# A Fourier-mixing and expert-layer kernel: the planner may hold back VectorE, ScalarE and GpSimd work, any free bank is taken, tile rows are turned in place, h comes in half tiles

## The chip, the cores and the metric

The kernel runs on one core of one Trainium2 chip. The metric is device microseconds of one execution. Three runs of the kernel before gave 1494.55, 1497.58 and 1498.59 us, median 1497.58.

## The reference

```python
X = np.fft.rfft(x, axis=1)                    # x: 8 batches, 2496 positions, 256 columns, float32
Y = X * (filt_r + 1j * filt_i)[None, :, :]
y = np.fft.irfft(Y, n=2496, axis=1)
x = y.reshape(19968, 256)                     # one row per token
logits = x @ w_gate                           # 8 experts
expert_idx = np.argmax(logits, axis=1)
gate_w = softmax(logits)[row, expert_idx]
h = np.maximum(x_of_expert @ w1[e], 0.0)      # 256 -> 1024, each row through its own expert only
out = gate_w[:, None] * (h @ w2[e])           # 1024 -> 256
```

## The kernel before

**The transform.** 2496 = 39 x 64, so each batch is transformed in four stages of matrix products. Stage A (`stage_a`) transforms along 39 with the table `ta` (three blocks of 39 positions on 117 partitions become three blocks of 40 values on 120 partitions); stage B (`stage_b`) transforms along 64 with `tb`, after which VectorE multiplies by the filter; stage C (`stage_c`) goes back along 64 with `tc`; stage D (`stage_d`) goes back along 39 with `td`. Between A and B, and between C and D, the data goes through DRAM (`zd`, `ud`) to be laid out anew, but for the first batch, which is turned on the chip (`first_a`, `turn_z`, `first_c`, `turn_u`). A batch is read in chunks `CH` of up to four columns blocks (22 in all: five chunks of four and one of two). A matmul has 512 columns (two blocks of 256), and its result lies in one of seven PSUM banks (`bank`) until VectorE or ScalarE copies it out (`evac`).

**The routing.** The output `yo` of stage D is turned, multiplied by the gate weights (`turn_y`, then `logits` and `turn_logits` for the first three batches, `block_logits` and `block_back` for the others), and `route` finds each token's expert, its place in that expert's list and its gate. GpSimd then writes each token's row, with its number and gate, into that place of a table `rowsd` in DRAM by indirect DMA (`scatter`), one DMA for the tokens of one block, on up to 117 partitions.

**The experts.** `tile_map` cuts the lists into tiles of 512, 256 or 128 rows. For a tile, `rows_in` loads the rows into `xg`, `turn_x` turns them on VectorE into another tile `xT`, `hidden` (or `hidden_by_quarters`, which does seven products in place of eight, with sums made by GpSimd in `turn_x` and `w1_sums`) makes h in the tile `hT`, and `result` multiplies by w2, scales by the gate and writes the rows of the output by indirect DMA. One `hT` tile holds h of half an expert's w1 columns, and there are three of them.

**The order.** All engines' queues are filled by a planner that runs while the program is built. `Order` keeps an estimated clock for each engine; every instruction goes through `Issue`, which advances the clocks and issues at once, so the line of every instruction in the profile is L238. A main loop picks, by estimated readiness, the next step for TensorE from the list of transform steps (`slot`) or from two streams of expert products (`first_products`, `second_products`, with `when` giving their readiness). After each step it lets stores go (`flush`), issues loads (`more_loads`, `prefetch`), and takes up to four pieces of routing (`side`). For a copy out of a bank, `either` picks VectorE or ScalarE by which would end first, and the copy is put in that engine's queue at once. Buffers, banks too, are taken in rotation (`Slots`). Instructions of one engine execute in the order of its queue.

Of the kernel before, what the change touches and what calls it, by code (L numbers as in the profile page):

```python
# [34 lines left out]
TK = NB * NS  # L35
DH = D // P
# [4 lines left out]
NJ = D // CT  # L41

# [13 lines left out]
def dft_tables():  # L56
# [25 lines left out]
    ids = np.zeros((NB, N1, NG))  # L82
    valid = np.zeros((NB, N1, NG))
    for j in range(NB):
        for i in range(len(range(j, N2, NB))):
            ids[j, :, i] = token(q, NB * i + j)
            valid[j, :, i] = 1.0

    by_block = np.zeros((4, CT, NG + 2))
    by_block.reshape(P, NG + 2)[:TP, :NG] = valid.reshape(TP, NG)  # L90
# [5 lines left out]
        "ta": ta.reshape(TP, TK),  # L96
        "tb": tb,
        "tc": tc,
        "td": np.pad(td.reshape(TK, TP), ((0, 0), (0, P - TP))),
        "sg": np.concatenate([sg[:, :NF // 2], sg[:, NF // 2:]]),  # L100
        "ids": ids.reshape(TP, NG),
        "valid": np.concatenate([np.pad(valid.reshape(TP, NG), ((0, P - TP), (0, 0))), by_block], axis=1),
    }


def lay_x(x):

    out = np.zeros((x.shape[0], P, NG, D), x.dtype)
    q = np.arange(N1)
    for j in range(NB):  # L110
        for i in range(len(range(j, N2, NB))):
            out[:, j * N1:(j + 1) * N1, i] = x[:, token(q, NB * i + j)]
    return out
# [11 lines left out]
class Order:  # L125
# [3 lines left out]
    LOAD = 2.0  # L129

    def __init__(self, nc):
        self.nc = nc
        self.t = dict.fromkeys(("tensor", "vector", "scalar", "gpsimd", "sync", "transfers"), 0.0)
        self.slow = self.busy = self.last = 0.0
        self.done, self.used, self.slots, self.ahead = {}, {}, {}, {}
        self.tensor, self.vector, self.scalar, self.gpsimd, self.sync = (
            Issue(self, name) for name in ("tensor", "vector", "scalar", "gpsimd", "sync"))
# [6 lines left out]

    def ready(self, *aps):
        times = [a for a in aps if isinstance(a, float)]
        return max([0.0] + times + [self.done.get(key, 0.0) for a in aps if not isinstance(a, float) for key in self.parts(a)])
# [29 lines left out]
    def count(self, engine, op, args, named):  # L177
        aps = [a for a in list(args) + list(named.values()) if isinstance(a, bass.AP)]
        if not aps:
            return  # L180
# [6 lines left out]
        at = named.get("out_offset")  # L187
        if at is not None:
            ins.append(at.ap)
        kept = [a for a in ins if a.space != DRAM or a.name[:2] in ("zd", "ud")]  # L190
        free = self.t[engine]
        start = max([free] + [self.ready(a) + (self.HOP if engine != "sync" else 0.0) for a in kept])
        if out is not None:
            start = max(start, self.ahead.pop(out.name, 0.0))
            n = int(np.prod([d[1] for d in out.ap][1:])) if out.space != DRAM else 0
        tail = 0.0
        if op.endswith("dma_start"):
            busy = 1.3 if engine == "gpsimd" else 0.4
            self.t[engine] = start + busy
            took = self.transfer(out, named["in_"])  # L200
            self.t["transfers"] = max(self.t["transfers"], start + busy) + took
            end, tail = self.t["transfers"], self.LOAD
        else:
            if out is None:
                took = 0.02
            elif engine == "tensor":
                if start > self.busy + 1.2:
                    self.slow = start + 3.4
                rows = out.ap[0][1]
                took = max(0.1, 0.00085 * n) if op == "transpose" else max(0.216, 0.00169 * n) if rows > 32 else 0.00045 * n  # L210
                took *= 2.0 if start < self.slow else 1.0
                tail = 0.25
            elif engine == "vector":
                took = 0.15 + n / 960
            elif engine == "scalar":
                took = 0.16 + n / 1200
            else:
                took = 0.2 + n / 480
            end = self.t[engine] = start + took
            if engine == "tensor":  # L220
                self.busy = end
# [4 lines left out]
        self.last = end + tail  # L226


class Issue:
# [3 lines left out]
    def __getattr__(self, op):  # L233
        real = getattr(getattr(self.order.nc, self.name), op)

        def issue(*args, **named):
            self.order.count(self.name, op, args, named)
            return real(*args, **named)  # L238

        return issue  # L240


class Slots:
    def __init__(self, order, pool, bufs):
        self.order, self.pool, self.bufs, self.tiles, self.n = order, pool, bufs, {}, {}

    def free(self, tag, k=0):

        past, n = self.tiles.get(tag, []), self.n.get(tag, 0)
        if len(past) + k < n or k >= n:  # L250
            return 0.0
        name = past[k - n]
        return max(self.order.done.get(name, 0.0), self.order.used.get(name, 0.0)) + 0.1

    def tile(self, shape, dtype, **named):
        new = self.pool.tile(shape, dtype, **named)
        past = self.tiles.setdefault(named.get("tag") or named.get("name"), [])
        n = self.n[named.get("tag") or named.get("name")] = named.get("bufs") or self.bufs
        if len(past) >= n:
            name = past[-n]  # L260
            self.order.ahead[new.name] = max(self.order.done.get(name, 0.0), self.order.used.get(name, 0.0)) + 0.1
        past.append(new.name)
        return new


@with_exitstack
def kernel(
# [39 lines left out]
    TR = E * TE  # L307

# [16 lines left out]
    prow = perm.tile([P, 1], I32, name="prow")  # L325
    need = perm.tile([1, 1], I32, name="need")
    ps = open_pool(ctx, name="ps", bufs=7, space=PSUM)

# [4 lines left out]

    tas = cst.tile([TP, TK], F32, name="tas")
    tbs = cst.tile([P, P], F32, name="tbs")
    tcs = cst.tile([P, P], F32, name="tcs")
    tds = cst.tile([TK, P], F32, name="tds")
# [15 lines left out]
    ids0 = cst.tile([TP, NG], F32, name="ids0")  # L353
    vld = cst.tile([P, 2 * NG + 2], F32, name="vld")
# [8 lines left out]
    def experts_pool():  # L363
        first.close()
# [8 lines left out]
    def either(i, n, on_vector, on_scalar):  # L373

        ready = nc.ready(i)
        if max(t["vector"], ready) + 0.15 + n / 960 <= max(t["scalar"], ready) + 0.16 + n / 1200:
            on_vector()
        else:
            on_scalar()

    def evac(o, i, n):
        either(i, n, lambda: nc.vector.tensor_copy(o, i), lambda: nc.scalar.copy(out=o, in_=i))
# [8 lines left out]
    def load_filters(c):  # L391
        f0, n = FH[c]
        if c == 0:
            nc.sync.dma_start(out=tbs, in_=tb)
# [11 lines left out]
        if c == 0:  # L406
            nc.sync.dma_start(out=tcs, in_=tcm)

    def load_rest():
        nc.sync.dma_start(out=tds, in_=td)  # L410
# [33 lines left out]
    def columns(ap, i0, n):  # L444
# [3 lines left out]
        yield TK, slice(0, m), rows[i0 * TK:(i0 + m) * TK, :].rearrange("(i p) d -> p i d", p=TK)  # L448
        if m < n:
            yield NS, slice(m, n), rows[(NG - 1) * TK:, :].rearrange("(i p) d -> p i d", p=NS)  # L450

    ins, outs, lgs, yts, lands = {}, {}, {}, {}, []
    NIN, YB = 7, 6
# [17 lines left out]
    def by_part(ap):  # L471

        return ap.rearrange("t (c f) d -> (t c) f d", c=2)

# [8 lines left out]
    def load_z(b, c):  # L483
        f0, n = FH[c]
        zi = fin(("z", b, c))
        nc.sync.dma_start(out=zi[:, :n], in_=by_part(zd[b])[:, f0:f0 + n, :])

    def load_u(b, c):
        i0, n = CH[c]
        ui = fin(("u", b, c))  # L490
        for r, m, v in columns(ud[b], i0, n):
            if r == TK:

                v = bass.AP(v.tensor, v.offset, [[D, P]] + [list(k) for k in v.ap[1:]])
                r = P
            nc.sync.dma_start(out=ui[:r, m], in_=v)

    def stage_a(b, c):
        i0, n = CH[c]
        xt = ins.pop(("x", b, c))  # L500
        zo = sb.tile([TK, 4, D], F32, tag="st", name="zo", bufs=4)
        for j in range(0, n, 2):
            p = bank()
            mm(p[:TK, :], lhsT=tas, rhs=xt[:TP, j:j + 2, :], start=True, stop=True)
            evac(zo[:, j:j + 2, :], p[:TK, :].rearrange("p (t d) -> p t d", t=2), 512)
        for r, m, v in columns(zd[b], i0, n):
            move(v, zo[:r, m])
# [3 lines left out]
    def stage_b(b, f):  # L511
# [6 lines left out]
        mm(p, lhsT=tbs, rhs=zi[:, j:j + 2, :], start=True, stop=True)  # L518
# [9 lines left out]
        if b == 0 or b < 3 and not sides:  # L528
            nc.gpsimd.tensor_tensor(ys, ys, yw, op=ALU.add)
        else:  # L530
            nc.vector.tensor_tensor(ys, ys, yw, op=ALU.add)

    def stage_c(b, f):
# [6 lines left out]
        mm(p, lhsT=tcs, rhs=ys, start=True, stop=True)  # L540
        evac(uo[:, j:j + 2, :], p.rearrange("p (i d) -> p i d", i=2), 512)
        if j == 2:
            f0 = f - 2
            move(by_part(ud[b])[:, f0:f0 + 4, :], uo)
# [3 lines left out]
    def stage_d(b, c):  # L548
# [8 lines left out]
        for j in range(0, n, 2):  # L557
            p = bank()
            if i0 + j + 2 < NG:
                mm(p, lhsT=tds, rhs=ui[:TK, j:j + 2, :], start=True, stop=True)  # L560
            else:

                for i, k in enumerate((TK, NS)):
                    mm(p[:, i * D:(i + 1) * D], lhsT=tds[:k, :], rhs=ui[:k, j + i, :], start=True, stop=True)
            evac(yo[:, j:j + 2, :D], p.rearrange("p (i d) -> p i d", i=2), 512)

# [824 lines left out]
```

## Time and profile before

| | |
|---|---|
| median of the three runs | 1497.58 us |
| the profiled execution | 1494.36 us |
| its span, from the first to the last instruction | 1492.7 us |
| mean granted TensorE clock | 0.991 |
| TensorE busy, matmuls | 1451.7 us, 97% |
| VectorE, ScalarE, GpSimd busy | 770.7, 471.8, 733.4 us |
| mean DMA rate | 186 GB/s |
| matmul records | 7396 |

PE is the matmul part of TensorE and PEld its weight loads, DVE is VectorE, ACT ScalarE, POOL GpSimd, SP SyncE, which issues most DMAs. A group of instructions is shown as engine, operation, output<-inputs, shape, count, then its busy time, the mean time of one in ns, and the idle time of the engine just before it with what ended it. Matmul durations overlap, since the next one starts before the last one's end; the distance from start to start tells what one costs. A matmul of float32 appears as two records. A wait line names who waited, for whom, us in total, number of times, and the longest.

### The profile page before, as it was taken

Reading aid. Unit: us, or ns where it says so; the run is one execution under the profiler, and the core shown is the slowest. Engines: PE = TensorE matmul, PEld = TensorE weight load, DVE = VectorE, ACT = ScalarE, POOL = GpSimd, SP = SyncE. Lnnn points to the kernel's source line nnn. Section 1 sums busy time; section 2 is a strip of 40 time slices with the busy share of each in tenths; the row PEclk is TensorE's granted clock in tenths of the full one; section 3 lists DMA queues with packets and bytes.
Section 4 is the critical chain, followed back from the end, with each engine's and each line's share of the span. In section 5 each row is a group of like instructions: output and inputs, shape, how many; then the busy total and the mean of one; then the engine's idle time right before and its main releaser. Section 6 shows DMA issues by size and latency. Waiting matters only on the chain. (4 is left out here: it accounts for less than half of the span.)

```text
span 1492.7 us, 24448 instructions
## 1 busy us (share of the span) xinstructions
PE 1451.7 (97%) x7396; PEld 1148.8 (77%) x7396; DVE 770.7 (52%) x1732; ACT 471.8 (32%) x983; POOL 733.4 (49%) x1053
## 2 busy tenths in 40 slices
PE   8898997999989999999999999999999999999998
PEld 6553555776667777777787888887888889999997
DVE  4667677354577656565764555537344334441110
ACT  4453442333322233222233222222222222223332
POOL 3434455344446656554555756764546455741111
PEclk9999999999999999999999999999999999999999
DMA  9749889678767756474456545545455543456661
GB/s 255 252 152 333 289 306 295 207 258 280 251 182 229 219 157 169 131 239 128 128 152 196 130 117 149 147 139 145 151 178 176 167 146 106 117 187 179 181 179 52
DMA packets 216376, 278.10 MB, mean 186 GB/s; under 512 B 124131, under 2 KB 163708, under 8 KB 216245
## 3 DMA queue, kind: packets, MB, share of 16 engines
q1 hardware_dynamic: 197125, 233.19, 52.7%
q0 software_dynamic: 19120, 43.33, 8.3%
q8 instruction: 62, 1.02, 0.3%
q14 instruction: 69, 0.57, 0.1%
HBM read 196.45 MB, written 80.64 MB: 186 GB/s over the span
## 5 line engine op out<-in xcount | busy, mean ns | idle before, releaser
L238 DVE TENSOR_TENSOR hT<-bank,hT 128x512 f32<-128x512 f32 (+1 forms) x504 | 300.7, 627 | 298.9 <-PE bank L238 183.1
L238 PE MATMUL bank<-w2t,hT 128*128 128x256 f32 x1984 | 447.5, 382 | 1.0 <-DVE hT L238 0.5
L238 PEld LDWEIGHTS bank<-w2t,hT 128*128 128x128 f32 x1984 | 377.6, 191 | 62.9 <-issue 9.5
L238 POOL DMA_INDIRECT out_dram<-ys,ng x161 | 160.7, 998 | 459.7 <-ACT ys L238 183.3
L238 PE MATMUL bank<-xT,w1t 128*128 128x256 f32 (+1 forms) x1728 | 316.7, 329 | 0.3 <-DVE xT L238 0.3
L238 PEld LDWEIGHTS bank<-xT,w1t 128*128 128x128 f32 x1728 | 266.8, 192 | 36.5 <-issue 11.8
L238 ACT ACTIVATE hT<-hT 128x1024 f32<-128x1024 f32 (+1 forms) x144 | 133.9, 958 | 378.7 <-DVE hT L238 374.8
L238 POOL DMA_INDIRECT rows<-yo,row x176 | 180.3, 1025 | 69.0 <-POOL yo L238 36.0
L238 ACT ACTIVATE ys<-bank,ng 128x256 f32<-128x256 f32 x128 | 60.6, 473 | 369.6 <-PE bank L238 297.0
L238 PE MATMUL bank<-sums,wsum 128*128 128x256 f32 (+1 forms) x576 | 135.7, 358 | 2.8 <-DVE hT L238 1.8
L238 PE MATMUL bank<-w2s,hT 128*128 x592 | 132.6, 380 | 0.0
L238 PEld LDWEIGHTS bank<-w2s,hT 128*128 128x128 f32 x592 | 110.5, 191 | 13.6
L238 PEld LDWEIGHTS bank<-sums,wsum 128*128 128x128 f32 x576 | 101.2, 191 | 20.1 <-issue 7.3
L238 DVE TENSOR_TENSOR ys<-bank,ht 128x512 f32<-128x512 f32 x80 | 55.0, 688 | 81.9 <-PE bank L238 77.3
L238 PE MATMUL bank<-fin,tas 117*120 117x512 f32 x154 | 76.9, 620 | 11.9 <-DMA fin<-in_x_dram 11.9
L238 PE MATMUL bank<-fin,tds 120*128 120x512 f32 (+1 forms) x168 | 76.6, 576 | 6.0 <-DMA fin<-ud 6.0
L238 DVE STREAM_TRANSPOSE xT<-xg 128x512 f32<-128x512 f32 (+2 forms) x126 | 57.5, 494 | 44.2 <-PE bank L238 44.2
L238 PE MATMUL bank<-fin,tbs 128*128 128x512 f32 x140 | 72.6, 605 | 2.5 <-DMA fin<-zd 2.5
L238 ACT ACTIVATE hT<-bank 128x128 f32<-128x128 f32 (+1 forms) x192 | 58.1, 304 | 50.1 <-PE bank L238 42.4
L238 PE MATMUL bank<-ys,tcs 128*128 128x512 f32 x140 | 72.7, 604 | 1.0 <-DVE ys L238 1.0
L238 POOL TENSOR_TENSOR wsum<-w1t 128x256 f32<-128x256 f32 x72 | 53.4, 742 | 38.1 <-PE bank L238 36.5
L238 PE MATMUL bank<-xT,wsum 128*128 128x256 f32 (+1 forms) x288 | 68.3, 360 | 0.3 <-DVE hT L238 0.3
(150 smaller groups left out, 1491.5 us busy)
## 6 DMA issues: line engine op xcount, KB each, us to landing
w1t<-in_moe_w_dram SPq DMA_DIRECT2D x126, 512.0 KB
w2t<-in_moe_w_dram SPq DMA_DIRECT2D x68, 512.0 KB
fin<-in_x_dram SPq DMA_DIRECT2D x39, 512.0 KB
fin<-zd SPq DMA_DIRECT2D x35, 512.0 KB
ud<-uo SPq DMA_DIRECT2D x35, 512.0 KB
fin<-ud SPq DMA_DIRECT2D x35, 512.0 KB
zd<-zo SPq DMA_DIRECT2D x35, 480.0 KB
xg<-rows SPq DMA_DIRECT2D x112, 128.0 KB
```

Of the source, the lines that this page charges most:

```text
L238: return real(*args, **named)
```

## The change

- **Holding.** An operation of VectorE, ScalarE or GpSimd is no longer issued at once but kept in a list, with the operations that it must follow. After each TensorE step, `advance` issues all held operations whose estimated start has come, earliest first. Where one can run on two engines (`one_of`: copies, relu, scaling on VectorE or ScalarE; the filter's sum on VectorE or GpSimd), the engine that would end it first is picked then. What an instruction of TensorE or SyncE needs is issued before it. The estimates now count a buffer as not free and a tile as not ready while a held operation touches it.
- **Buffers.** Banks and the transform's input tiles are taken where one is free first, not in rotation. Loads for the experts are issued only when a buffer is free within 0.5 us by the estimate (`soon`). `xg` has three buffers, not two.
- **Tile rows.** `turn_x` turns `xg` in place by one instruction in place of two; `xT` is gone, and matmuls and GpSimd's sums read the rows in pieces of 32.
- **h.** Six `hT` tiles of half the size in place of three. `result` takes the products in the order 0, 1, 4, 5, 6, 7, 2, 3, and may be picked 2.0 us before the third half tile is expected.
- **Stage D.** The tokens of one block lie on 124 partitions instead of 117. `stage_d` makes them by four matmuls of 64 output rows into two banks where it made two matmuls of 128 output rows. Rows without a token get an index past the table's end, which the indirect DMA skips.
- **Folded stages.** A form of stages A and D for batches from `BQ` on, with sums and differences (`fold_x`, `fold_y`). `BQ` is 8, and there are 8 batches. The second tables of `ta`, `tb` and `tc` for it are loaded near the end of the transform.
- GpSimd gets a small memset between two scatters that would stand next to one another (16 in the program).

The diff, cut to its core:

```diff
+    def given(self, engine, op, args, named):
+        if self.caught is not None:
+            self.caught.append((engine, op, args, named))
+            return None
+        if engine in self.HELD and self.hold:
+            self.held.append(Held(self, [(engine, op, args, named)]))
+            return None
+        out, ins = self.operands(op, args, named)
+        self.clear([key for a in ins for key in self.parts(a)], self.parts(out) if out is not None else [])
...
+        made = self.issue(engine, op, args, named)
...
+    def advance(self):
+        while True:
+            free = [(work.begin(), k) for k, work in enumerate(self.held) if not work.behind]
+            begin, k = min(free, default=(self.NEVER, 0))
+            if begin > self.t["tensor"]:
+                return
+            self.held[k].go()
...
     def free(self, tag, k=0):
         past, n = self.tiles.get(tag, []), self.n.get(tag, 0)
+        if tag in self.live:
+            return sorted(self.freed(name, tag) for name in past)[k] if past else 0.0
...
+        if tag in self.live:
+            past = self.tiles.setdefault(tag, [None] * n)
+            k = min(range(n), key=lambda k: self.freed(past[k], tag))
...
-        either(i, n, lambda: nc.vector.tensor_copy(o, i), lambda: nc.scalar.copy(out=o, in_=i))
+        nc.one_of(lambda: nc.vector.tensor_copy(o, i), lambda: nc.scalar.copy(out=o, in_=i))
...
-        if b == 0 or b < 3 and not sides:
-            nc.gpsimd.tensor_tensor(ys, ys, yw, op=ALU.add)
-        else:
-            nc.vector.tensor_tensor(ys, ys, yw, op=ALU.add)
+        sums(ys, ys, yw, ALU.add)
...
     def stage_d(b, c):
...
-        for j in range(0, n, 2):
-            p = bank()
-            if i0 + j + 2 < NG:
-                mm(p, lhsT=tds, rhs=ui[:TK, j:j + 2, :], start=True, stop=True)
-            else:
-                for i, k in enumerate((TK, NS)):
-                    mm(p[:, i * D:(i + 1) * D], lhsT=tds[:k, :], rhs=ui[:k, j + i, :], start=True, stop=True)
-            evac(yo[:, j:j + 2, :D], p.rearrange("p (i d) -> p i d", i=2), 512)
+        m, tds = n // 2, tables["td"]
+        both = [bank()[:, :m * D].rearrange("p (i d) -> p i d", i=m) for _ in range(2)]
+        for h in range(2):
+            last = i0 + n == NG and h == 1
+            for k in range(2):
+                if b < BQ:
+                    rows, cols = slice(0, NS if last else TK), slice(64 * k, 64 * k + 64)
...
+                mm(both[k][64 * h:64 * h + 64], lhsT=tds[rows, cols], rhs=ui[rows, h * m:(h + 1) * m, :], start=True, stop=True)
+        evac(yo[:, :m, :D], both[0], m * D)
+        if b < BQ:
+            evac(yo[:, m:n, :D], both[1], m * D)
...
+    def sums(o, i0, i1, op):
+        nc.one_of(*(lambda on=on: on.tensor_tensor(o, i0, i1, op=op) for on in (nc.vector, nc.gpsimd)))
...
     def turn_x(i):
-        xts[i] = pools["moe"].tile([P, DH, 4 * P], F32, tag="xT", name="xT", bufs=2)
-        for dh in range(DH):
-            nc.vector.transpose(xts[i][:, dh, :n * P].rearrange("p (g r) -> p g r", r=QW), xg[:, :n * NQ, dh, :])
+        xg = xg[:, :n * NQ]
+        nc.vector.transpose(xg, xg)
+        xts[i] = xg.rearrange("p g h r -> p h g r")
...
+    def new_hidden(i):
+        new = pools["moe"].tile([P, 2, 4 * P], F32, tag="hT", name="hT", bufs=6)
+        hs.setdefault(i, []).append(new)
+        return new
...
     def result(i, j):
-        for k in range(FT):
+        for m, k in enumerate((0, 1, 4, 5, 6, 7, 2, 3)):
...
+    def soon(tag):
+        return pools["moe"].free(tag) <= max(t["tensor"], t["sync"]) + 0.5
...
-            return max(ps.free("bank"), nc.ready(*hs[i], *((late["w2s"],) if i >= PLACE else (w2t[2 * i], w2t[2 * i + 1]))))
+            return max(ps.free("bank"), nc.expected(hs[i][2]) - 2.0, nc.ready(hs[i][0], hs[i][1], hs[i][3], *((late["w2s"],) if i >= PLACE else (w2t[2 * i], w2t[2 * i + 1]))))
```

## The prediction, made before the changed kernel ran

> **What bounds the kernel now.** First the page's busy lines and its slices: TensorE is busy for 97% of the span, in nearly every slice, and no other engine passes 52%.
>
> ```profile
> span 1492.7 us, 24448 instructions
> PE 1451.7 (97%) x7396; PEld 1148.8 (77%) x7396; DVE 770.7 (52%) x1732; ACT 471.8 (32%) x983; POOL 733.4 (49%) x1053
> ```
>
> So a better choice of engine for a copy pays only where TensorE stands still, and anything that TensorE does more costs its full price. Second, TensorE's waits in three stretches. They sum to 26.7 us before 260 us (20.8 of it for three kinds of transfers), 5.4 us from 260 to 1000 and 2.7 us after that. The longest are these:
>
> ```profile
> PE bank L238 <- DMA fin<-in_x_dram: 12.3, 6, 6.9
> PE bank L238 <- DMA fin<-ud: 6.0, 1, 6.0
> PE bank L238 <- DVE hT L238: 3.6, 4, 1.8
> PE lt L238 <- DVE yt L238: 3.1, 1, 3.1
> ```
>
> Third, the windows. At 120 to 140 us the DMA engines are full, TensorE is busy for 12.89 of 20 us and the granted clock falls to 0.83, so a wait costs more than itself; from 600 on nothing is left to win.
>
> ```profile
> core 0: us, PE busy (x) PEld busy (x) DVE busy (x) ACT busy (x) POOL busy (x), PEclk, DMA share, GB/s
> ...
> 120.00:140.00 20.00, 12.89 (x27) 5.32 (x26) 11.21 (x24) 6.52 (x15) 6.33 (x11) 0.83 1.02 342
> ...
> 600.00:800.00 200.00, 199.03 (x990) 157.50 (x990) 124.45 (x257) 56.40 (x106) 105.41 (x150) 1.00 0.53 155
> ```
>
> Fourth, two pieces of TensorE's timeline (start, duration, tile, records): one step of `stage_d`, and one visit of `block_logits`, whose matmuls write 32 rows each.
>
> ```profile
> 505.89 1.88 PE L238 MATMUL bank<-fin,tds 120*128 120x512 f32 x4
> 507.61 1.03 PE L238 MATMUL bank<-xT,wsum 128*128 128x256 f32 x4
> ...
> 539.63 1.03 PE L238 MATMUL bank<-sums,w1t 128*128 128x256 f32 x4
> 540.59 0.65 PE L238 MATMUL lt<-yt,wb 128*32 128x128 f32 x16
> 541.16 1.13 PE L238 MATMUL bank<-xT,wsum 128*128 128x256 f32 x4
> 542.13 1.24 PE L238 MATMUL bank<-xT,w1t 128*128 128x256 f32 x5
> ```
>
> Starts are to be read, not durations. A matmul leaves two records. The two matmuls of `stage_d` take 507.61 - 505.89 = 1.72 us, 0.43 a record of 512 columns; four records of 256 columns take 0.86, which makes 0.108 for 128 columns.
>
> **What the change moves, part by part.**
>
> *stage_d in half rows.* This is the one part that gives TensorE more work. A step's two matmuls of 128 output rows become four of 64 output rows (the column index k selects table columns, h the half of the output rows): eight records of 512 columns instead of four. The trace has no such step, so its price is bounded by rows on both sides.
> (a) Stream time, lower end: as now, 1.72 us, if the two halves of the array run at once; less is excluded, since each half still streams four records of 512 columns. The `lt` row is nearest: sixteen records of 128 columns, 16 x 0.108 = 1.73 us one by one, are through in 541.16 - 540.59 = 0.57 us, so the four column groups do run together.
> (b) Upper end: eight records one after another, 3.44 us. Forty steps of 1.72 and eight last ones of 0.86 give 75.7 us more.
> (c) Between: the order. In `lt` a column group's two records stand together and the next group's follow; in `stage_d` four records of one half come before the first of the other. If only one record may wait per half while a later one goes past it, the second half starts two records late: six steps instead of four, 0.86 x 40 + 0.43 x 8 = 37.8 us more.
> (d) Going into the split array and back. Around the `lt` visit, the four `sums,w1t` records take 0.96 us to the next start instead of 0.86, `lt` 0.57 instead of a quarter of 1.73 = 0.43, and the four `xT,wsum` after it 0.97 instead of 0.86: 0.10 + 0.14 + 0.11 = 0.35 us a visit. The order of the built kernel has 48 such steps; two stand together and six lie beside a 32-row visit, which saves one of their two changes of form, so about 44 count: 44 x 0.35 = 15.4 us.
> I take (a) with (d), since `lt` is the only split work on record; (b) and (c) stay for the range.
>
> [...]
>
> *More rows.* 132 transposes of 117 columns become 124 columns: 7 x 0.00084 x 132 = 0.8 us. The 66 `wg` matmuls grow as much on a quarter of the array, 0.2 us. With the shorter last step's extra evacuation nothing more than 0.3 us: together 1.3 us.
>
> *Tile rows turned in place.* On VectorE the big tile's two transposes of 686 ns become one; the row `yt<-yo 128x1024` has 1235 ns, so 137 ns less for 28 tiles, off TensorE's path. TensorE now reads the rows in pieces of 32 columns; `lt` already reads so (128 columns as 4 pieces of 32) at 0.43 / 4 = 0.108 us, no slower. GpSimd's sums on these pieces (0.73 us each) may get slower; each tile has four, GpSimd idles half the span, and the next tile is turned while two others are under way. If that cover were gone, 4 x 0.73 = 2.9 us a tile would show. I take nothing.
>
> *h in halves, and the second products reordered.* `result` now takes k as 0, 1, 4, 5, 6, 7, 2, 3 and may start 2.0 us before the third half tile is counted ready. Six products of 2 x 0.216 us, 2.6 us, come first, so 0.6 us is in hand. Where the planner is late by more, TensorE stops with both product streams behind it. Before, VectorE's `hT` cost it 3.6 us in four waits; a gain can be no more than that, a loss say 1 us for each of the 28 tiles of 512 rows. I take zero: VectorE's 686 ns and ScalarE's 1053 ns (1024 elements) are within 0.05 us of what the planner counts.
>
> *Held operations, any free bank, loads only into buffers soon free.* These move VectorE, ScalarE and GpSimd work (the built order puts 76 instead of 64 filter sums on VectorE, 29 instead of 11 output copies, and the scaling of results almost wholly on ScalarE), all under a busy TensorE. Their worth is bounded by the waits that other engines caused: 34.8 - 20.8 = 14.0 us in all, of which I take 4, since a new order makes waits of its own. Of the transfers' 20.8 us I take none as removed by order: in the built order `stage_d` of the second batch still follows directly on the last two `tc` matmuls whose result it reads back through DRAM, the 6.0 us wait. On SP, the three additional 64 KB table loads wait for the last reader of the first table and stand before loads planned well ahead; one 512 KB load's worth of issue is 0.4 us, so nothing. The scatters stay 176, at 1025 ns on GpSimd, where the bounded `out_dram` form has 998.
>
> *Where the extra work is hidden.* The first three batches' 18 visits, 6.3 us, fall before 260 us or soon after, where TensorE waits for transfers; half of it, 3 us, should vanish in those waits.
>
> **Sum.** The profiled execution took 1494.4 us (span 1492.7): 1494.4 + 15.4 + 1.3 - 4 - 3 = 1504.1. The median of the runs shown is 3.2 us above that execution, so 1507.
>
> **Rivals.**
> 1. *The halves don't run together* (c: one record waits; b: none overlaps). For it: four records of one half in a row, which no row shows. Against it: `lt` gets past waiting records. [...] It decides as soon as a step's next start is later than 2.1 us.
> 2. *Faster: the placement empties the early waits.* Place: 0 to 260 us and 430 us. Loads go out only when their buffer is about to be free, so SP is no longer held by a full buffer with an x or u load behind it. Price: the transfers' 20.8 us, 8 of the other waits and the low clock that follows them (0.83 for 20 us around the 6.0 us wait, some 3 us; 0.91 at 40 to 60), in all about 32; less 16.7 for the first two parts, 1497.6 - 32 + 16.7 = 1482; with two thirds of it, 1493. It decides from 21 us saved on. Against it: DMA share 1.02 in that window, so the bytes themselves bound it.
> 3. *Second products started too early*: 28 tiles at 1 us, 1535. Against it: the 0.6 us in hand.
> 4. *Part of the change doesn't act.* The folded form of stages A and D, with its fourfold split, is for batches from the eighth on, counted from zero, and there are eight: it never runs. So no product gets cheaper, which is in the sum already.
>
> **How the numbers follow.** Likeliest, the split with full overlap: 0.56, 1495 to 1519 by itself. Rival 1: 0.18 for six steps, 0.05 for more. Rival 2: 0.18. Rival 3: 0.03. The range of 1487 to 1546 leaves out rival 1's far end and the best of rival 2. A measurement of this kernel can tell about 0.3%, 4.5 us: below 1493.1 is rival 2 for the larger part and a small tail of the first case, 0.20; within, the lower third of the first case, 0.16; above, the rest, 0.64.
>
> **What would show it.** The group `fin,td` with 64 output rows and 280 records of 512 columns; a step that runs to the next start in about 1.72 + 0.35 us, right, or 2.6 and more, rival 1. TensorE's busy time up by some 12 to 17 us with waits near 30 us: right. Waits below 15 us and the clock at 1.0 in all early windows: rival 2. Waits on `hT` after 1000 us above 10 us: rival 3. The time from 1000 us to the end should stay what it was; if that stretch moves by more than 5 us, the reading that TensorE alone sets it is wrong.

## The result: slower by 2.5%, and the profile after

The changed kernel takes 1534.26 us (median of 1528.97 to 1538.76) against 1496.07 us for the kernel before: a ratio of 1.0255, 95% interval 1.0215 to 1.0295. The profiled execution is the lowest of the four, 1528.97 us. The forecast of 1507 us is 27 us too low; the range of 1487 to 1546 us holds the result.

The head of the profile page of the changed kernel, then three of its groups (busy time in us, mean of one in ns, idle time before, and what ended it):

```profile
span 1527.3 us, 25038 instructions
PE 1477.9 (97%) x7588; PEld 1142.1 (75%) x7588; DVE 763.0 (50%) x1635; ACT 492.2 (32%) x1043; POOL 772.8 (51%) x1057
...
q0 software_dynamic: 33456, 43.58, 9.7%
...
L306 POOL DMA_INDIRECT out_dram<-ys,ng x161 | 160.1, 994 | 404.1 <-ACT ys L306 165.1
...
L306 POOL DMA_INDIRECT rows<-yo,row x176 | 238.9, 1357 | 72.9 <-POOL yo L306 40.0
...
L306 PE MATMUL bank<-fin,td 120*64 120x512 f32 (+1 forms) x336 | 86.9, 592 | 15.2 <-DMA fin<-ud 10.0
```

TensorE is busy 26 us more than before. The scatters of tile rows take 1357 ns each on average where they took 1025, while the other indirect transfer of GpSimd still takes 994. They also make more packets: the software queue, which is GpSimd's, has 33456 where it had 19120.

TensorE's waits sum to 43 us, against 34.8 before. The longest groups, in us in total, times, and longest:

```profile
PE bank L306 <- DMA fin<-ud: 10.0, 2, 7.6
PE bank L306 <- issue: 8.5, 1, 8.5
PE bank L306 <- DMA fin<-in_x_dram: 8.4, 4, 4.8
PE bank L306 <- ACT yo L306: 6.6, 2, 5.2
```

The windows of the changed kernel (columns as before) show two stretches with long waits that the kernel before did not have, at 300 and at 850 us, each with a lower granted clock. After 1000 us TensorE is busy nearly throughout in both kernels.

```profile
300.00:320.00 20.00, 11.55 (x48) 9.67 (x48) 5.81 (x31) 3.79 (x12) 15.59 (x21) 0.81 0.63 177
850.00:900.00 50.00, 42.43 (x213) 30.95 (x212) 21.70 (x52) 12.86 (x26) 31.17 (x45) 0.90 0.64 187
1000.00:1400.00 400.00, 399.02 (x2129) 358.71 (x2128) 165.16 (x337) 113.39 (x200) 214.47 (x291) 1.00 0.52 156
```

TensorE's timeline of the changed kernel has a full step of `stage_d` and the short step that ends a batch (two blocks, records of 256 columns):

```profile
340.19 1.94 PE L306 MATMUL bank<-fin,td 120*64 120x512 f32 x8
342.06 1.78 PE L306 MATMUL bank<-xg,w1t 128*128 128x256 f32 x7
...
381.25 2.08 PE L306 MATMUL bank<-fin,td 120*64 120x256 f32 x8
383.26 1.13 PE L306 MATMUL bank<-fin,tb 128*128 128x512 f32 x2
```

The full step takes 342.06 - 340.19 = 1.87 us to the next start, against 1.72: its two halves run together. The short step, half the work, takes 383.26 - 381.25 = 2.01 us. Eight records of 256 columns at 0.215 one after another make 1.72 us. The other 0.29 us lies at the first and the last record of each half, which take 0.27 and 0.31 us to the next start where the others take 0.216: nothing overlaps. Both its halves have 64 output rows, but the first reads 120 rows of the table and the second only 40, since no token lies beyond them.

The wait at 308 us is read from four queues of the changed kernel: TensorE's matmuls, SP's loads with the one wait that SP has from 290 to 318 us, VectorE and GpSimd.

```profile
304.58 3.62 PE L306 MATMUL bank<-xg,w1t 128*128 128x256 f32 x16
316.65 3.75 PE L306 MATMUL bank<-xg,w1t 128*128 128x256 f32 x8 [8.45 <-issue]
```

```profile
290.71 0.33 SPq L306 DMA_DIRECT2D w2t<-in_moe_w_dram  x1
307.35 1.95 SPq L306 DMA_DIRECT2D xg<-rows  x4
309.49 0.40 SPq L306 DMA_DIRECT2D ng<-rows  x1
311.00 1.79 SPq L306 DMA_DIRECT2D w1t<-in_moe_w_dram  x2
```

```profile
SPq L306 <- DMA rows<-yo,row: 15.3, 1, 15.3
```

```profile
305.44 0.20 DVE L306 TENSOR_REDUCE rs<-ex 124x6 f32<-124x48 f32 x1 [18.28 <-POOL yo L306]
```

```profile
303.38 0.19 POOL L306 COPY yo<-rs 124x8 f32<-124x8 f32 x1
303.87 1.34 POOL L306 DMA_INDIRECT rows<-yo,row  x1 [0.30 <-POOL yo L306]
305.22 0.19 POOL L306 COPY yo<-rs 124x8 f32<-124x8 f32 x1
305.71 1.33 POOL L306 DMA_INDIRECT rows<-yo,row  x1 [0.30 <-POOL yo L306]
```

SP issues nothing from 291 to 307 us, because the load of expert rows must follow the scatters that write those rows. A load of w1 stands behind it in SP's queue and goes out at 311. The profile names no releaser for TensorE's wait ("issue"); the matmuls that end it at 316.65 read `xg` and `w1t`, and the rows in `xg` were turned by 312.6, so the load of w1 is what is left to wait for. GpSimd meanwhile writes a scatter every 1.84 us (305.71 - 303.87), and VectorE waits 18.28 us before it can overwrite the gates in `rs`, which GpSimd is still copying. So the engine that seemed to have half its time free, and the transfers that it starts, stand ahead of TensorE's loads here.

### The profile page after: what moved, and what is told of

Same layout as the page of the kernel before. It is cut to its first block, busy times and chain, and to the rows that moved or that the text cites. A ratio compares the mean times of both kernels' runs of the same rounds, so it can differ in the third digit from the quotient of the medians.

```text
span 1527.3 us, 25038 instructions
## 1 busy us (share of the span) xinstructions
PE 1477.9 (97%) x7588; PEld 1142.1 (75%) x7588; DVE 763.0 (50%) x1635; ACT 492.2 (32%) x1043; POOL 772.8 (51%) x1057
## 3 DMA queue, kind: packets, MB, share of 16 engines
q0 software_dynamic: 33456, 43.58, 9.7%
## 5 line engine op out<-in xcount | busy, mean ns | idle before, releaser
L306 PE MATMUL bank<-xg,w1t 128*128 128x256 f32 (+1 forms) x1728 | 318.1, 330 | 8.5 <-issue 8.5
L306 PEld LDWEIGHTS bank<-xg,w1t 128*128 128x128 f32 x1728 | 267.3, 192 | 45.8 <-issue 21.8
L306 POOL DMA_INDIRECT rows<-yo,row x176 | 238.9, 1357 | 72.9 <-POOL yo L306 40.0
L306 ACT ACTIVATE ys<-bank,ng 128x256 f32<-128x256 f32 x160 | 75.9, 474 | 421.5 <-PE bank L306 344.0
L306 PEld LDWEIGHTS bank<-w2s,hT 128*128 128x128 f32 x592 | 109.7, 190 | 13.4
L306 DVE STREAM_TRANSPOSE xg<-xg 128x1024 f32<-128x1024 f32 (+2 forms) x63 | 53.6, 851 | 131.7 <-DMA xg<-rows 93.9
L306 PE MATMUL bank<-fin,td 120*64 120x512 f32 (+1 forms) x336 | 86.9, 592 | 15.2 <-DMA fin<-ud 10.0
L306 PE MATMUL bank<-fin,ta 117*120 117x512 f32 x154 | 75.4, 608 | 7.8 <-DMA fin<-in_x_dram 6.4
L306 PE MATMUL bank<-fin,tb 128*128 128x512 f32 x140 | 75.4, 624 | 4.1 <-DMA fin<-zd 4.1
L306 PE MATMUL bank<-ys,tc 128*128 128x512 f32 x140 | 72.5, 604 | 0.0
L306 PEld LDWEIGHTS bank<-fin,td 120*64 120x64 f32 x336 | 26.3, 141 | 59.1 <-issue 38.3
```

The source lines that it names most:

```text
L306: return getattr(getattr(self.nc, engine), op)(*args, **named)
```

## The experiments

The kernel before ran again beside each set; its medians are 1495.0 to 1495.7 us. Ratios are to those runs. Of each diff the lines that matter are shown.

**1. Full rows.** Stage D as before, everything else as changed.

```diff
-YR = 64 + TH
+YR = TP
...
-                mm(both[k][64 * h:64 * h + 64], lhsT=tds[rows, cols], rhs=ui[rows, h * m:(h + 1) * m, :], start=True, stop=True)
...
+                mm(p, lhsT=tds[:TK], rhs=ui[:TK, j:j + 2, :], start=True, stop=True)
```

> The changed kernel with stage_d alone put back: two matmuls of 128 output rows a step, tokens on 117 partitions, so no matmul of stage_d works on half of the array; the choice among held operations, any free bank, tile rows turned in place, half h tiles and the bounded scatter stay. Theory (the split's changes of form and its serial short steps are most of the loss): 0.35 us for each of about 49 visits, 17.2 us, and 1.16 us for each of 8 short steps, 9.3 us, go; from 1534 us to about 1508, TensorE's busy time down by some 15 to 26 us, waits as in the changed kernel (about 43 us). Rival (the holding and the new order of loads make the loss by waits): it stays above 1520, with waits above 45 us.

1479.79 us, ratio 0.9908 (0.9885 to 0.9930): faster than both kernels, and twice the fall that was expected. TensorE's waits sum to 20.7 us:

```profile
PE bank L300 <- DMA fin<-in_x_dram: 8.3, 6, 3.2
PE bank L300 <- DMA fin<-ud: 3.4, 3, 1.6
PE bank L300 <- DMA fin<-zd: 2.6, 1, 2.6
```

So stage D in half rows, with all that hangs on it, costs 54 us, and the rest of the change gains 15. The rival that blamed the holding falls. The price that was expected for TensorE's own work (17.2 + 9.3) explains only half of the 54.

**2. Split alone.** The kernel before, with each matmul of stage D cut into two halves of the array. Orders are equal on all engines but TensorE's own pairs.

```diff
-                mm(p, lhsT=tds, rhs=ui[:TK, j:j + 2, :], start=True, stop=True)
...
+            for h in range(2):
+                at = slice(64 * h, 64 * h + 64)
+                if i0 + j + 2 < NG:
+                    mm(p[at], lhsT=tds[:, at], rhs=ui[:TK, j:j + 2, :], start=True, stop=True)
```

> The kernel before with one edit: each matmul of stage_d with 128 output rows becomes two of 64 output rows on the two halves of the array, into the same bank and from the same table; the order on every engine stays. The last, short steps keep halves of equal form (same rows of the table for both). Theory: only the change into and out of the split array is paid, about 0.35 us for each of some 88 steps or 44 neighbouring pairs (two steps often stand together): 15 us at 44 visits, so 1496 to about 1512; the fin,td pairs start some 13 ns apart. Rival (the halves do not run together unless the second half's matmul is of another bank, or in program order only): six steps instead of four, 38 us or more, 1534 and above. If the split costs nothing by itself, it stays at 1496.

1505.01 us, ratio 1.0069 (1.0050 to 1.0089): 10 us, less than the 15 expected. TensorE is busy 14.4 us more and waits 3.4 us less. One step in its timeline, with what stands beside it:

```profile
512.45 1.03 PE L239 MATMUL bank<-sums,w1t 128*128 128x256 f32 x4
513.41 1.94 PE L239 MATMUL bank<-fin,tds 120*64 120x512 f32 x8
515.27 1.13 PE L239 MATMUL bank<-xT,wsum 128*128 128x256 f32 x4
516.24 1.89 PE L239 MATMUL bank<-xT,w1t 128*128 128x256 f32 x8
```

Eight records of 512 columns run to the next start in 1.86 us where four took 1.72, and the groups of four on either side take 0.96 and 0.97 us instead of 0.86. The halves run together, and going into the split array and back is what is paid.

**3. Equal halves in the short step.** The changed kernel, with 120 table rows in both halves; one small load more in each batch fills the additional input rows.

```diff
-                    rows, cols = slice(0, NS if last else TK), slice(64 * k, 64 * k + 64)
+                    rows, cols = slice(0, TK), slice(64 * k, 64 * k + 64)
```

> The changed kernel with the last, short step of stage_d made of two equal halves: the second half's matmuls use all 120 rows of the table, as the first half's do, instead of 40 (80 more partitions of the input tile are loaded with other rows, whose products go to rows that are not used; one small load more a batch). Theory (a matmul on 40 rows and one on 120 rows do not run at the same time, so the short step runs one matmul after another): the short step goes from 2.01 us to about 1.2 us to the next start, 8 steps, 6 to 9 us less: 1534 to about 1526. Rival (the 64-column halves with 256 moving columns are serial whatever their rows): no change, 2.0 us a step.

1518.04 us (1510.69 to 1527.14), 16 us less than the changed kernel. Its timeline has the short step at 379.28 - 378.26 = 1.02 us instead of 2.01:

```profile
378.26 1.09 PE L306 MATMUL bank<-fin,td 120*64 120x256 f32 x8
379.28 1.13 PE L306 MATMUL bank<-xg,w1t 128*128 128x256 f32 x4
```

Eight steps, each 0.99 us shorter, make 7.9 us. What the median fell beyond that is not traced: the planner's order differs a little here, and single runs of this kernel spread over 16 us.

**4. Nothing held.** The changed kernel, one word changed.

```diff
-        self.held, self.hold, self.caught = [], True, None
+        self.held, self.hold, self.caught = [], False, None
```

> The changed kernel with nothing held: VectorE, ScalarE and GpSimd operations are issued at once, in the program's order, each to the engine that the planner picks at that moment; half rows, any free bank, in-place turn and half h tiles stay. If holding makes the additional waits (43 us in the changed kernel against 35 before), some 8 us go: about 1526, split work unchanged (1.87 us a full step, 2.01 us a short one). If holding is what keeps the smaller h tiles and the in-place turn cheap, waits grow, above all on hT, yt and ut: 1545 or more. If it does nothing: 1534.

1563.53 us, ratio 1.0464 (1.0444 to 1.0485): 29 us more. TensorE's waits go from 43 to 66 us, most of the rise on other engines' work:

```profile
PE bank L306 <- ACT yo L306: 10.0, 3, 5.7
...
PE bank L306 <- POOL wsum L306: 6.7, 3, 4.2
```

The theory that holding makes the additional waits falls; it removes waits.

**5. Scatters of 128 rows.** After the trace of experiment 1 the suspicion moved to GpSimd's scatters: full rows have the same bounds check, yet 1005 ns a scatter at the median. The changed kernel, with four more rows in each scatter (`SR` is 128):

```diff
-            rows.append((row[:YR, i:i + 1], yos[i // 4][:YR, i % 4, :]))
+            rows.append((row[:SR, i:i + 1], yos[i // 4][:SR, i % 4, :]))
```

> The changed kernel with one edit: GpSimd's 176 scatters of tile rows take 128 rows each instead of 124 (the four more are out of bounds and write nothing; three small memsets more). The order on every other engine is that of the changed kernel. In the trace of the changed kernel each scatter takes 1336 ns at the median; with 117 rows, as before and in the run with full rows, 1005 ns, although both have the bounds check; other indirect transfers of 128 rows take 990 ns. Theory (the number of rows, 124, makes the scatter dear, and the queue of GpSimd holds VectorE and then SP's loads, which is the 8.5 us wait at 308 us and more): about 1000 ns a scatter, the 8.5 us wait gone or under 3 us, TensorE's waits from 43 to about 25 us, 1534 to about 1515. Rival (scatters are off the path): scatter cheaper or not, the time stays at 1530 and above. Rival 2 (out-of-bounds rows among the valid ones make it dear): still 1336 ns, no change.

1502.06 us, 32 us less, ratio to before 1.0054 (1.0036 to 1.0073). Two lines of its page:

```profile
q0 software_dynamic: 16560, 43.32, 7.9%
...
L307 POOL DMA_INDIRECT rows<-yo,row x176 | 178.8, 1016 | 68.3 <-issue 23.4
```

More rows, a cheaper scatter, half the packets. TensorE's waits fall from 43 to 21.5 us; the wait at 308 us becomes one of 4.0, that at 873 us one of 1.1.

**6. Both repairs.** Experiments 3 and 5 together.

> The run with equal halves in the short step (1518 us) with scatters of 128 rows as well. If the two costs are apart and the second is worth some 15 to 19 us: about 1500. What is left over the run with full rows (1480) would then be the changes of form of the split, 10 to 17 us. If the scatters are off the path: 1518.

1488.91 us, ratio 0.9950 (0.9931 to 0.9969): better than expected, and a little faster than before although stage D is split. It is 13 us below experiment 5; TensorE's busy time falls by 7.4 us of these (1469.8 to 1462.4), near the 7.9 by the starts. It lies 9 us above experiment 1, which is what the split and the additional rows still cost here.

**7. Full rows with the split.** Experiment 1 with the edit of experiment 2.

> The run with full rows (1480 us: held operations, any free bank, in-place turn and half h tiles, but tokens on 117 partitions) with each matmul of stage_d split into two of 64 output rows into the same bank, the order on every engine as in that run. Theory: the split alone costs the 10 us that it cost in the kernel before (1505 against 1495), here about 1490, with 117-row scatters at 1005 ns and waits as in the run with full rows (22 us). Rival (the planner's tighter order has no slack left, so late halves turn into waits): 1500 or more, waits above 35 us.

1494.04 us, 14 us above experiment 1. The split's own price is thus 10 us in the old order and 14 in the new; its waits sum to 20.6 us, as there (20.7), and TensorE is busy 13.4 us more. Its short step pairs halves of equal form, two of 120 rows and then two of 40:

```profile
348.99 1.23 PE L300 MATMUL bank<-fin,td 120*64 120x256 f32 x8
350.15 1.13 PE L300 MATMUL bank<-xg,w1t 128*128 128x256 f32 x4
```

It takes 1.16 us where the changed kernel's takes 2.01. So halves that read 40 rows overlapped too where both did; what kept them apart in the changed kernel was the unequal form.

**8. Scatters of 124 rows, full rows.** Experiment 1 with seven more rows, all out of bounds, in each scatter: the edit of experiment 5 with `SR` 124.

> The run with full rows (1480 us) with one edit: its scatters take 124 rows instead of 117 (the seven more are out of bounds and write nothing; three small memsets more), the order on every other engine unchanged. Theory (the number of rows sets the price): 1336 ns a scatter instead of 1005, software-queue packets from 19,400 to about 33,000, and, since GpSimd's queue holds VectorE and SP, waits up by 10 to 20 us: 1490 to 1500. Rival (half rows as such make the scatter dear): 1005 ns, 1480. Rival 2 (dear but off the path): 1336 ns, 1480.

1511.80 us, 32 us above experiment 1, the same as the fall in experiment 5 and more than the 1490 to 1500 expected. Stage D is untouched here. One line of its page:

```profile
L301 POOL DMA_INDIRECT rows<-yo,row x176 | 237.6, 1350 | 71.6 <-POOL yo L301 36.9
```

TensorE's waits sum to 38.7 us, 18 more than in experiment 1, and its busy time rises by 10 us (1448.2 to 1458.4) for the same matmuls, with a mean granted clock of 0.988 instead of 0.994. So the number of rows in a scatter, and neither the split nor the bounds check, is worth 32 us.

**9. Scatters of 128 rows, full rows.** Experiment 1 with the edit of experiment 5.

> The run with full rows (1480 us) with scatters of 128 rows instead of 117 (the eleven more are out of bounds and write nothing; three small memsets more), the order on every other engine unchanged: the candidate for the fastest version. In the changed kernel 128 rows brought the scatter to 984 ns at the median, against 1005 ns for 117 rows: 176 x 21 ns, 4 us of GpSimd's time. Theory (GpSimd's queue counts, but 21 ns a scatter is little): 1476 to 1480. If landing times matter more than the issue: below 1474.

1480.17 us, ratio 0.9887 (0.9866 to 0.9908), no different from experiment 1. Going from 117 to 128 rows wins nothing.

**10. Full rows, nothing held.** The edits of experiments 1 and 4.

> The run with full rows (1480 us) with nothing held: VectorE, ScalarE and GpSimd operations are issued at once in the program's order. With half rows, dropping the holding cost 29 us (1534 to 1563). Theory (holding is what makes the rest of the change a gain: 15 us against the kernel before): 1495 to 1510, with TensorE's waits 15 to 25 us above the 22 us of the run with full rows. Rival (with scatters at 1005 ns GpSimd's queue is short enough for any order, and the gain is from the half h tiles, the in-place turn and the loads): within 5 us of 1480.

1493.66 us, ratio 0.9991 (0.9975 to 1.0007), 14 us above experiment 1, just short of the 1495 expected; TensorE waits 37.2 us instead of 20.7. With good scatters, the choice among held operations is worth 14 us, and all the rest (any free bank, in-place turn, half h tiles, later loads) together nothing that can be measured.

**11. Other row counts.** Experiment 8 with another count for each batch.

> The run with full rows, with another number of rows in the scatters of each batch: 118, 119, 120, 121, 122, 123, 125 and 126 for the eight batches in turn (the rows above 117 are out of bounds and write nothing). It measures GpSimd's time for 22 scatters of each count; the time of the whole is of no interest. So far 117 rows take 1005 ns, 128 take 984, 124 take 1336. Theory A (124 is dear because its largest divisor up to 16 is small: 4, where 117 has 13 and 128 has 16): 120 (15) and 126 (14) about 1000, 121 (11) near that, 119 (7), 125 (5), 123 (3), 118 and 122 (2) 1200 and more. Theory B (dear above some number of rows that is not a multiple of 16): all counts from 118 or some higher one on take about 1336. Theory C (multiples of 4 are bundled differently): 120 and 124 dear, the others about 1000.

GpSimd's scatters in the eight stretches of time, for 118, 119, 120, 121, 122, 123, 125 and 126 rows in turn (after x22: duration in ns, lowest, median, highest):

```profile
L301 POOL DMA_INDIRECT rows<-yo,row x22: 1647/1656/1882, 89.5 to 157.5; - x22
...
L301 POOL DMA_INDIRECT rows<-yo,row x22: 1087/1098/1585, 183.9 to 226.4; - x22
...
L301 POOL DMA_INDIRECT rows<-yo,row x22: 1001/1012/1084, 259.8 to 311.6; - x22
...
L301 POOL DMA_INDIRECT rows<-yo,row x22: 1019/1032/1166, 332.0 to 414.8; - x22
...
L301 POOL DMA_INDIRECT rows<-yo,row x22: 1674/1688/1760, 440.8 to 544.2; - x22
...
L301 POOL DMA_INDIRECT rows<-yo,row x22: 1414/1422/1941, 607.1 to 716.5; - x22
...
L301 POOL DMA_INDIRECT rows<-yo,row x22: 1193/1213/1496, 758.0 to 864.2; - x22
...
L301 POOL DMA_INDIRECT rows<-yo,row x22: 987/1002/1083, 882.1 to 966.6; - x22
```

Put by the largest divisor up to 16, with the counts of the other runs, the medians fall, but for 120 rows:

| rows | largest divisor up to 16 | ns |
|---|---|---|
| 118, 122 | 2 | 1656, 1688 |
| 123 | 3 | 1422 |
| 124 | 4 | 1336 |
| 125 | 5 | 1213 |
| 119 | 7 | 1098 |
| 121 | 11 | 1032 |
| 117 | 13 | 1005 |
| 126 | 14 | 1002 |
| 120 | 15 | 1012 |
| 128 | 16 | 984 |

(120 rows take 10 ns more than 126, less than the spread of either.) Theory A holds for these counts. Put another way, by the rows over that divisor (8 at 128, 31 at 124, 61 at 122), the median rises by about 13 ns for each of them, (1688 - 984) / (61 - 8); that line meets every other count within 28 ns but 124, which lies 46 above it. Why the divisor decides was not shown: the trace names no single DMA engine.

**12. GpSimd's time without the slow scatter.** Experiment 5, and after each scatter a write that nothing reads.

```diff
+        if op == "indirect_dma_start" and named["in_"].name[:2] == "yo":
+            self.nc.gpsimd.memset(self.idle, 0.0)
```

> The run of the changed kernel with scatters of 128 rows (1502 us, 984 ns a scatter), and after each of the 176 scatters an idle write of GpSimd (a memset of 128x288 elements of a tile that nothing reads, about 350 ns by the 333 ns of the memset of 128x272), which the planner does not count: GpSimd spends on each scatter what it spent with 124 rows, 1336 ns, but the scatter itself is the cheap one. The order on the other engines is the same. Theory (GpSimd's queue time is what 124 rows cost: its delay goes on to VectorE, SP and the loads): back up by most of the 32 us, 1525 to 1535, TensorE's waits near 45 us. Rival (what costs is how late the 124-row scatter's data land): 1502 to 1508, waits near 25 us.

1506.35 us (1502.73 to 1512.22), 4 us above experiment 5. Its timeline shows a scatter every 1.75 us; in experiment 5 it is every 1.46, in the changed kernel every 1.84:

```profile
294.28 0.99 POOL L307 DMA_INDIRECT rows<-yo,row  x1 [0.28 <-POOL yo L307]
295.27 0.35 POOL L309 MEMSET idle<- 128x288 f32 x1
...
296.03 0.99 POOL L307 DMA_INDIRECT rows<-yo,row  x1 [0.28 <-POOL yo L307]
```

Three quarters of the additional time in GpSimd's queue bring back an eighth of the 32 us, and hardly more than 8 us if the spread of both sets of runs is allowed for. Most of what 124 rows cost is therefore not GpSimd's time but what comes after it, in the transfers. One part of that is in the traces. At 850 us SP waits for the rows of the same scatter in each kernel. The scatter and SP's load after it, in the changed kernel and then in this one:

```profile
862.47 1.33 POOL L306 DMA_INDIRECT rows<-yo,row  x1 [0.30 <-POOL yo L306]
867.06 1.93 SPq L306 DMA_DIRECT2D xg<-rows  x4
```

```profile
849.35 0.99 POOL L307 DMA_INDIRECT rows<-yo,row  x1 [0.28 <-POOL yo L307]
851.99 1.93 SPq L307 DMA_DIRECT2D xg<-rows  x4
```

The load goes out 867.06 - 863.80 = 3.26 us after the scatter of 124 rows has ended on GpSimd, but 851.99 - 850.34 = 1.65 us after the one of 128 (1.63 in experiment 5). At six more such waits the distance is 3.6 to 3.9 us in the changed kernel and 1.5 to 1.7 in the other two. So the rows of a slow scatter also land some 2 us later, and SP's waits for scatters sum to 179.4 us in the changed kernel, 148.3 here and 111.9 in experiment 5. How much of the 32 us these later rows make, and whether other loads were held up as well, was not measured.

## Why the prediction was right and wrong

**The sum of the parts, by measured medians:**

| part | predicted, us | measured, us |
|---|---|---|
| holding, banks, loads, in-place turn, half h tiles | -4 | -15 (experiment 1), of which holding -14 (10) |
| split: into the array and back, (a) with (d) | +15.4 | +14 (7), +10 (2), +9 with the additional rows (6 against 1) |
| last, short steps | within (a) | +13 to +16 by medians (6 against 5, 3); +7.9 by the starts |
| scatters | 0 | +32 (5, 8) |
| more rows, work hidden in early waits | +1.3, -3 | not separated |

Undone one after another, the parts are -15 (experiment 1), +9 (6 against 1), +13 (5 against 6) and +32 (the changed kernel against 5): 39 us, against 38 measured for the whole. That sum closes by itself, since each part is the distance to the next run. With the 14 of experiment 7 for the split it would be 44: the parts share waits, and what one is worth depends on the others. Of the 13 for the short steps, the traces account for some 8.

**Right: the price of the split.** The step runs to the next start in 1.87 us, as (a) has it, with about 0.1 us more on each side, as (d) has it. Six steps in place of four, as in (c), would have taken 2.6 us, and eight, as in (b), 3.44. Experiments 2, 6 and 7 put the price at 9 to 14 us. Trusting the `lt` row was right. Rival 1 falls with it, although its time, 1507 + 38 = 1545 us by (c), came nearer than the forecast: a time near a rival's says nothing for its mechanism. That the range holds 1534 is luck in the same way: its upper end stood for rival 1, and what fills the gap is a term that the sum put at nothing.

**Wrong, and the step that failed: "The scatters stay 176, at 1025 ns on GpSimd".** The count was looked at and the number of rows was not, although the part on more rows prices the 124 columns of the transposes. Both rows that bounded the price, 117 rows at 1025 ns and 128 rows at 998, are counts with a divisor of 13 and 16. The new count lies between them and costs more than either: a price between two rows is no bound when it depends on something other than size. The term stood at nothing in the sum, and the scatters cost 32 us. GpSimd's 58 us of additional time are the smaller part of that, some 4 us by experiment 12; the larger part comes after it. The rows land some 2 us later (SP's loads of them go out 3.3 to 3.9 us after the scatter's end instead of 1.5 to 1.7), these loads must follow them, and TensorE's loads stand behind those in SP's queue.

**Wrong: the last steps.** (b) named "eight last ones of 0.86", and (a) let them overlap like the others. But only their first half reads 120 table rows. In the trace the two forms did not overlap: 2.01 us a step, against 1.02 with equal halves. Why unequal forms stayed apart was not shown. What was measured is that they did, and that two halves of 40 rows ran together (1.16 us a step, experiment 7).

**Mis-sized: the held operations.** The bound was 14.0 us, the waits that other engines caused, and 4 were taken for "a new order makes waits of its own". Holding is worth 14 (experiment 10). With full rows TensorE waits 14 us less than before, 20.7 against 34.8, and 6.5 of these lie in the three kinds of transfers, which were put at none: their waits fall from 20.8 to 14.3. Half of rival 2's 32 us is thus there, but not by its mechanism, the later loads, alone: with these loads and nothing held (experiment 10) the same waits still sum to 18.9. In the changed kernel the scatters buried the gain.

**The rest.** Rival 3 falls: waits on `hT` are 1.0 us. The stretch from 1000 us to the end was to stay what it was, and is 35 us longer (527.3 us against 492.7). That is work put off, not waiting: it holds 2951 matmul records instead of 2778, and TensorE waits 1.0 us in it instead of 2.7. A mark in microseconds was the wrong sign, and the reading that TensorE alone sets this stretch stands. Of what was to show the forecast, the waits "near 30 us" and the busy time "up by some 12 to 17 us" failed (43 and 26). With the cheap scatters of experiment 5 they are 21.5 and 18, and with equal short steps as well (experiment 6) 22.0 and 11, so it was there that they failed.

## What to carry to other kernels

Before a tile's row count changes, look at every transfer that takes its shape from it: a scatter of 124 rows was dearer here than one of 117 or of 128, and 32 us hung on it. When work is split over the array, check that the last, partial piece keeps the tile form of the others: here the short step took 2.01 us with two forms and 1.02 with one. Undo the one part that touches shapes first: of a change that lost 2.5%, everything else was a gain of 1%, at 1480 us.

## What the runs showed of the hardware that was not expected

- A scatter's time on GpSimd went by the largest divisor up to 16 of its row count, over the eleven counts run here: 984 ns at 16, 1336 at 4, 1656 and 1688 at 2. Rows that are out of bounds showed no price of their own: seven more of them at 124 rows were dear (1337 ns, experiment 8), eleven more at 128 were free (981 ns, experiment 9), against 1005 ns without them.
- Two matmuls of 64 output rows ran together when both read 120 rows (1.02 us for eight records of 256 columns) or both read 40 (1.16 us for a step with a pair of each), and one after the other when one read 120 and the other 40 (2.01 us).
- The end of the scatter on GpSimd is not the end of its price: idle writes that make its cycle 0.29 us longer cost 4 us in all, where the slow scatter, 0.38 us longer a cycle, came with 32. Its rows were there for SP 3.3 to 3.9 us after it had ended on GpSimd, those of the fast one after 1.5 to 1.7.
